# Unread products, mask steps and weight loads at the beginning of a DeltaNet and SwiGLU kernel

## Chip, core and metric

The kernel runs on one core of a Trainium2 chip. The metric is the device time of one execution in microseconds (us). The engines are named as in the profile: PE (TensorE), DVE (VectorE), ACT (ScalarE), POOL (GpSimd) and SP (SyncE, which here issues the DMAs).

## What is computed

```python
# deltanet: q, k, v of (4, 8, 768, 48), beta of (4, 8, 768)
k_n = k / (np.linalg.norm(k, axis=-1, keepdims=True) + 1e-06)
for t in range(S):
    y[:, :, t] = einsum('bhd,bhde->bhe', q[:, :, t], state)
    v_old = einsum('bhde,bhd->bhe', state, k_n[:, :, t])
    state = state + beta_t * einsum('bhd,bhe->bhde', k_n[:, :, t], v[:, :, t] - v_old)
# its output becomes x of (3072, 384); then the block with d_ff = 1536
g = x @ w_gate
out = (g / (1 + exp(-g)) * (x @ w_val)) @ w_out
```

All inputs and outputs are float32.

## The kernel before

The sequence of 768 is cut into 12 chunks of 64 positions; a chunk holds all 32 heads. For each chunk K and Q are transposed on PE (`turned`, L481), Gram products are formed (`gram_steps`, L497; `first_gram`, L638, for the first two), a small triangular matrix is inverted by substitution on DVE, and `advance` (for chunk 0 `first_advance`) applies it to V, updates the state and gives the chunk's output y. The 256 tokens of a chunk then go through the SwiGLU block: `gate_val` (products L1440, SiLU on ACT L1449, product on DVE L1451) and `output` (L1467) for the first two chunks, and forms with fewer products (L1280, L1557) for the others.

The change lies in the beginning, about the first 60 us. There chunks 0 and 1 are prepared and advanced while the weights come in. The program's order is written out by hand for all five engines, at the end of the kernel.

**Unread products.** `unread(count, p)` (L631) puts `count` products of a constant tile `half` into PSUM tile `p`, 512 columns each; nobody reads them. Before the change they stand at the very start (3) and ahead of `first_substitution` in PE's order (2). A float32 product is two weight loads and two product records in the trace.

**The first chunk.** `first_advance` has four product steps of L932, written into the banks px and py: zt with v, then n_of with v, n_of with uu, n_of with t. Between them ACT copies v and uu (L957, L967) and DVE adds into t and uu (L1510). Then come the products with `p_sb`, copies into y (L1004, L1006), transposes of y (L1018), and `of_state` (L902). `n_products` (L728) precedes them.

**Masks.** `p_sb` of chunk 0 is the Gram product of q and k (copied by ACT, L517), multiplied by a triangular mask on POOL in two halves (`under_mask`, L536). The generator `first_q[0]` yields before each half, and `next(first_q[0])` places them.

**Weight loads.** `stage(n, after)` loads piece n of the weights through SP's queue (L267). With `after` it first copies one element of piece `after` into the place of n on POOL (L266). So the load of n waits until piece `after` has landed, and POOL's queue waits with it. Pieces 0 to 23 have 256 columns of the gate and value weights, 256 KB each. `load_v` and `load_k` go through the same queue of SP.

**Conversions.** `power_step` reads a landed piece on ACT (L279, L285); `convert` finishes it on DVE with three instructions (L296, L304, L316). For the first two `gate_val` of chunk 0, `chain` stands behind each group of three products: it takes one step of `advance(1)` and converts a few pieces. `advance(1)` forms products with the state (L1054) that DVE subtracts from v (L1064), products of q (L1044), then L1073, three times L1098, `of_state` (L902) and `p_of_u` (L1127), each step between groups of L1440.

Of the kernel before, what the change touches and what calls it, by code (L numbers as in the profile page):

```python
# [13 lines left out]
C = 64  # L14
DP = 64
R = 32
# [4 lines left out]
def kernel(  # L21
# [25 lines left out]
    nc = tc.nc  # L47
# [131 lines left out]
    def load_v(c):  # L179
        vin[c] = work.tile([128, 2, NB, NJ, D], FP32, name="vin", bufs=2)  # L180
        for b in range(2):
            src = halves(v, c, b).rearrange("bp (j par) p d -> par p (bp j) d", par=2)
            for par in range(2):
                s = half_of(b ^ par if c > 1 else b).start
                nc.sync.dma_start(
                    out=vin[c][s : s + 64, par].rearrange("p bp j d -> p (bp j) d"),
                    in_=src[par],
                )
# [170 lines left out]
    def half_of(x):  # L359
        return slice(64 * x, 64 * x + 64)  # L360
# [182 lines left out]
    def gram(*args):  # L543
        for _ in gram_steps(*args):
            pass
# [82 lines left out]
    def unread(count, p):  # L628

        for _ in range(count):  # L630
            nc.tensor.matmul(p[0:R], half, half[:, 0:1].to_broadcast([128, 512]))  # L631

    def first_gram(c, tag):

        p_v = [p.rearrange("p (x h i) -> p x h i", x=2, i=R) for p in banks("p_g", tag)]
        for bp, j, par, b, _ in every():
            k_v = kt[c][half_of(par), bp, j, b].rearrange("p (x i) -> p x i", x=2)
            nc.tensor.matmul(  # L638
                p_v[par][half_of(b), :, NJ * bp + j], kt[c][half_of(par), bp, j, b], k_v
            )  # L640
        return p_v
# [66 lines left out]
    def spread_z(c, x, engine, bps=slice(0, NB)):  # L708

        def by_bp(t):  # L710
            t = t.rearrange("p (par bp j) i -> p par bp j i", par=2, bp=NB)[:, :, bps]
            return t.rearrange("p par bp j i -> p par (bp j) i")

        z_v = by_bp(first_of["z"].rearrange("p i (c h) -> p c h i", c=2)[:, c])
        out = by_bp(ztp[0][:, c, :, R * x : R * x + R])
        mask = m_rows[:, 1:2] if x else m_rows[:, 3:4]
        if engine is nc.scalar:
            nc.scalar.mul(out, z_v, mask)
        else:
            engine.tensor_scalar_mul(out, z_v, mask)  # L720
# [200 lines left out]
    def first_advance():  # L921

        zt = ztp[0][:, 0].rearrange("p (par bp j) i -> p par bp j i", par=2, bp=NB)
        r, pq = vin.pop(0), p_sb.pop(0)
        p_n = banks("p_n", 2)
        n_products(0, p_n)
        n_copies(0, p_n, (nc.scalar.copy, nc.vector.tensor_copy), nc.vector.tensor_copy)

        def product(p, at, flip, weights, moving):
            for j in range(NJ):  # L930
                for par, b in ORDER:
                    nc.tensor.matmul(  # L932
                        p[half_of(b ^ par if flip else b), at[par], j],
                        weights(par, b, j),
                        moving(par, b, j),
                    )

        def there(par, b):
            return half_of(b ^ par)

        v, uu = new_u("v0"), new_u("uu")
        t = x_flat.rearrange("p (x bp j d) -> p x bp j d", x=3, bp=NB, j=NJ)
        pairs = [
            ps_pair("p_u", tag)[:, :, 0 : NJ * D].rearrange("p x (j d) -> p x j d", j=NJ)
            for tag in ("px", "py")
        ]
        n_of = n_sb[0]
        back_of = n_back[0].rearrange("p (bp j i) -> p bp j i", bp=NB, j=NJ)
        for bp in range(NB):
            product(  # L950
                pairs[bp],
                (1, 0),
                True,
                lambda par, b, j: zt[half_of(b), par, bp, j],
                lambda par, b, j: r[half_of(b), par, bp, j],
            )
            nc.scalar.copy(v[:, :, bp], pairs[bp])  # L957
        yield MORE
        for bp in range(NB):
            product(  # L960
                pairs[bp],
                (0, 1),
                False,
                lambda par, b, j: n_of[there(par, b), par, bp, j],
                lambda par, b, j: v[there(par, b), 1 - par, bp, j],
            )
            nc.scalar.copy(uu[:, :, bp], pairs[bp])  # L967
        yield MORE
        for bp in range(NB):
            product(  # L970
                pairs[bp],
                (1, 0),
                True,
                lambda par, b, j: (
                    back_of[half_of(b), bp, j] if par else n_of[half_of(b), 0, bp, j]
                ),
                lambda par, b, j: uu[half_of(b), par, bp, j],
            )
            plus(t[:, 0:2, bp], v[:, :, bp], pairs[bp])
            for x in range(2):  # L980
                nc.scalar.copy(t[half_of(x), 2, bp], t[half_of(1 - x), 0, bp])
        yield MORE
        for bp in range(NB):
            product(
                pairs[bp],
                (0, 1),
                False,
                lambda par, b, j: n_of[there(par, b), par, bp, j],
                lambda par, b, j: t[there(par, b), 1 - par, bp, j],
            )  # L990
            plus(uu[:, :, bp], t[:, 1:3, bp], pairs[bp])
        spread_z(1, 0, nc.vector)
        load_v(2)
        yield
        y = work.tile([128, NB, NJ, 2, D], FP32, name="y", tag="r", bufs=2)
        for bp, copy in enumerate((nc.scalar.copy, nc.vector.tensor_copy)):
            product(
                pairs[bp],
                (0, 1),
                True,  # L1000
                lambda par, b, j: pq[half_of(b), par, bp, j],
                lambda par, b, j: uu[half_of(b), par, bp, j],
            )
            copy(y[:, bp, :, 0], pairs[bp][:, 0])  # L1004
            for b in range(2):
                copy(y[half_of(b), bp, :, 1], pairs[bp][half_of(1 - b), 1])  # L1006
        yield
        y_f = y.rearrange("p bp j par d -> p bp (j par d)")
        xts[0] = x_first
        p_f = [  # L1010
            p[:, 0 : KT * 128].rearrange("p (t n) -> p t n", t=KT)
            for p in banks("p_f", 2)
        ]
        x_v = x_first.rearrange("p t (bp n) -> p t bp n", bp=NB)
        for bp, copy in enumerate((nc.scalar.copy, nc.vector.tensor_copy)):
            for k in range(KT):
                at = slice(k * 128, (k + 1) * 128)
                nc.tensor.transpose(p_f[bp][:, k], y_f[:, bp, at], ident)  # L1018
            copy(x_v[:, :, bp], p_f[bp])
        p_s = of_state(0, uu)  # L1020
        spread_z(1, 1, nc.scalar)
        nc.scalar.copy(state, p_s)
        yield
# [485 lines left out]
    def plus(out, a, b):  # L1509
        nc.vector.tensor_tensor(out=out, in0=a, in1=b, op=ALU.add)  # L1510
# [296 lines left out]
    with tc.manual_schedule(  # L1807
# [28 lines left out]
        nc.vector.transpose(first_of["mb"][:, 0 : R * R], first_of["flat"])  # L1836
        r_b = first_n()
        first_scale(r_b)
        for n in range(6):
            stage(n, n - 2 if n > 1 else None)  # L1840
        load_v(1)
        turned(2, False, "py")
        first_q = [gram_steps(0, True, 0, (copy_a, copy_a))]
        next(first_q[0])
        low_copies(0, p_g[0])
        turned(3, False, "py")
        turned(1, True, "px")
        gram(2, False, "py", (copy_a, copy_a))
        low_copies(1, p_g[1])
        gram(3, False, "py", (copy_a, copy_a))  # L1850
        first_q.append(gram_steps(1, True, "px", (copy_a, copy_a)))
# [9 lines left out]
        spread_z(0, 1, nc.vector, others)  # L1861
        scale_v(0)
        next(first_q[1])
        stage(6, 4)
        next(first_q[0])
        stage(7, 5)
        next(first_q[0])
        for n in range(8, 10):
            stage(n, n - 2)
        for n in range(10, 18):  # L1870
            stage(n, n - 3)
        for n in range(18, 23):
            stage(n)
        zb_1 = work.tile([128, R, R], FP32, name="zb", bufs=1)
        new_nt(0, spare_of_q, state.rearrange("p b bp j d -> p (b bp j d)")[:, 0:512])
# [22 lines left out]
        went = []  # L1898

        def chain(_):  # L1900

            if not went:
                p_n = banks("p_n", 0)
                n_products(1, p_n)
                n_copies(1, p_n, (copy_a, copy_a), copy_a)
            step("advance", advance, 1)
            n, ahead = ((1, 7), (2, 6), (4, 4))[len(went)] if len(went) < 3 else (2, 4)
            went.append(n)
            if len(went) in (4, 5):
                next(first_q[1])  # L1910
            convert(todo[:n], ahead)
            del todo[:n]

        pairs = [(c, f) for c in range(2) for f in range(0, 8, 2)]
        pairs += [(c, f) for f in range(8, FT, 2) for c in range(2)]
# [69 lines left out]
```

## Time and profile before

| | |
|---|---|
| median of 3 runs | 687.34 us (686.76 to 689.09) |
| profiled execution, its own time | 689.76 us |
| profiled execution, span | 688.1 us |
| mean granted TensorE clock | 0.992 |
| PE busy | 653.7 us (95%) |
| DVE, ACT, POOL busy | 473.3, 256.1, 201.7 us |

The profiled execution's own time is 1.7 us longer than the span from its first to its last instruction, and 2.4 us above the median of the runs. In the profile a row gives start and duration in us, the engine, the line of the kernel, the operation with its tiles, the number of instructions merged in the row, and in brackets how long the engine had been idle and what ended that. "issue" there means that the engine waited for nothing that the profile shows.

### The profile page before, as it was taken

What the parts mean: (1) busy time and instruction counts of PE and PEld (TensorE: products, weight loads), DVE (VectorE), ACT (ScalarE), POOL (GpSimd) and SP (SyncE); (2) the same over time, 40 slices, a digit from 0 to 9 for tenths busy, and PEclk for the clock granted to TensorE, in tenths of its full rate; (3) what the DMA queues carried; (4) which work ended last, traced back from release to release, by engine and by line L of the source; (5) the groups of instructions that cost most, each with busy time, mean ns of one, the idle gap of its engine ahead of it and who ended that gap; (6) DMA issues with size and microseconds to landing.
All of it is one profiled execution on the core that took longest, in us unless ns stands there. A gap on an engine that the chain in (4) does not pass through costs nothing.

```text
span 688.1 us, 24813 instructions
## 1 busy us (share of the span) xinstructions
PE 653.7 (95%) x10850; PEld 603.7 (88%) x10850; DVE 473.3 (69%) x982; ACT 256.1 (37%) x546; POOL 201.7 (29%) x309
## 2 busy tenths in 40 slices
PE   7788999998999999999999999999999999999997
PEld 4566888756988899999999999999999999999997
DVE  7987778798569867757767747767657655645462
ACT  5785765214332332334332244332232333132130
POOL 7130031104883030881030881030882000000000
PEclk9998999999999999999999999999999999999999
DMA  9767824016226352276262176242187122132220
GB/s 135 169 176 190 243 94 137 1 35 136 45 45 164 73 136 64 49 156 143 54 134 74 45 153 138 60 110 80 26 171 152 48 88 78 40 100 71 76 71 23
DMA packets 147437, 68.55 MB, mean 100 GB/s; under 512 B 123457, under 2 KB 126561, under 8 KB 147329
## 3 DMA queue, kind: packets, MB, share of 16 engines
q1 hardware_dynamic: 144992, 66.48, 40.2%
q8 instruction: 85, 1.39, 0.8%
q10 hardware_dynamic: 2080, 0.39, 0.4%
q0 software_dynamic: 256, 0.10, 0.1%
q14 instruction: 24, 0.19, 0.1%
HBM read 59.08 MB, written 7.86 MB: 97 GB/s over the span
## 4 chain that ended last, share of the span: by engine, by line
PE 64%; DVE 3%; issue 0%; DVEq 0%
PE ffn L1280 36%; PE ffn L1557 17%; PE p_px L1073 1%; PE p_px L1054 1%; PE p_py L497 1%; PE p_py L1127 1%; PE p_py L1044 1%; DVE x_t L1510 1%; DVE ffn L1507 1%; PE p_px L902 1%; PE p_px L497 1%; PE p_py L1152 1%; PE p_py L884 1%; PE p_px L870 1%; DVE o_sb L1510 0%
## 5 line engine op out<-in xcount | busy, mean ns | idle before, releaser
L1280 PE MATMUL ffn<-x_t,w_gv 128*128 128x128 f32 x760 | 102.4, 278 | 6.6 <-DVE x_t L1507 6.6
L1280 PEld LDWEIGHTS ffn<-x_t,w_gv 128*128 128x128 f32 x760 | 93.1, 193 | 8.3 <-issue 5.8
L1557 PE MATMUL ffn<-wo_sb,h_f 128*128 128x192 f32 x480 | 84.2, 329 | 0.6 <-ACT ffn L1549 0.6
L811 POOL TENSOR_TENSOR n_b<-mb,half 128x32 f32<-128x32 f32 x5 | 27.6, 5520 | 191.3 <-DVE mb L551 191.3
L1280 PE MATMUL ffn<-x_ffn,w_gv 128*128 128x128 f32 x600 | 80.0, 277 | 0.0
L1557 PEld LDWEIGHTS ffn<-wo_sb,h_f 128*128 128x128 f32 x480 | 77.8, 190 | 1.6 <-ACT ffn L1549 0.9
L1316 ACT ACTIVATE sil<-ffn 128x256 f32<-128x256 f32 x95 | 34.5, 382 | 114.6 <-PE ffn L1280 106.6
L586 POOL TENSOR_TENSOR zb<-zb,h_f 128x31 f32<-128x31 f32 (+15 forms) x124 | 71.9, 580 | 9.7
L1280 PEld LDWEIGHTS ffn<-x_ffn,w_gv 128*128 128x128 f32 x600 | 73.8, 194 | 0.0
L580 POOL TENSOR_TENSOR h_f<-zb,mb 128x31 f32<-128x31 f32 (+15 forms) x124 | 69.4, 560 | 14.4 <-DVE mb L568 5.0
L1280 PE MATMUL ffn<-x_t,h_f 128*128 128x128 f32 x464 | 63.6, 280 | 3.9 <-DVE ffn L1507 3.9
L1317 DVE TENSOR_TENSOR h_f<-sil,ffn 128x256 f32<-128x256 f32 x95 | 37.6, 418 | 42.8 <-ACT sil L1316 42.8
L1280 PEld LDWEIGHTS ffn<-x_t,h_f 128*128 128x128 f32 x464 | 56.3, 192 | 5.9 <-DVE ffn L1507 4.9
L1440 PE MATMUL ffn<-x_ffn,w_gv 128*128 128x256 f32 x216 | 48.0, 381 | 0.0
L1440 PEld LDWEIGHTS ffn<-x_ffn,w_gv 128*128 128x128 f32 x216 | 40.7, 190 | 5.6
L1510 DVE TENSOR_TENSOR o_sb<-o_sb,ffn 128x192 f32<-128x192 f32 x49 | 17.1, 349 | 31.5 <-PE ffn L1557 31.0
L1510 DVE TENSOR_TENSOR ffn<-ffn,p_sb 128x512 f32<-128x512 f32 x36 | 24.8, 693 | 16.2 <-PE ffn L1280 15.1
L1557 PE MATMUL ffn<-last_k,h_f 128*128 128x192 f32 x200 | 35.8, 326 | 0.0
L1440 PE MATMUL ffn<-x_t,w_gv 128*128 128x256 f32 x144 | 35.7, 400 | 0.0
L1557 PEld LDWEIGHTS ffn<-last_k,h_f 128*128 128x128 f32 x200 | 32.8, 190 | 0.0
L1440 PEld LDWEIGHTS ffn<-x_t,w_gv 128*128 128x128 f32 x144 | 27.7, 199 | 4.0
L1280 PE MATMUL ffn<-x_ffn,h_f 128*128 128x128 f32 x224 | 30.0, 277 | 0.0
(343 smaller groups left out, 1165.2 us busy)
## 6 DMA issues: line engine op xcount, KB each, us to landing
h_f<-w_s SPq DMA_DIRECT2D x81, 256.0 KB, 2.7
more_w<-w_s SPq DMA_DIRECT2D x27, 256.0 KB, 2.9
vin<-in_v_dram SPq DMA_DIRECT2D x48, 96.0 KB, 3.5
out_dram<-o_sb SPq DMA_DIRECT2D x48, 96.0 KB, 2.2
kn<-in_k_dram SPq DMA_DIRECT2D x20, 192.0 KB, 4.7
w_s<-h_f SPq DMA_DIRECT2D x10, 256.0 KB, 3.2
zt<-in_moe_w_out_dram SPq DMA_DIRECT2D x6, 384.0 KB, 4.4
qpad<-in_q_dram SPq DMA_DIRECT2D x36, 64.0 KB, 3.2
```

Of the source, the lines that this page charges most:

```text
L497: nc.tensor.matmul(p_v[par][half_of(b if of_q else b ^ par), bp, j], kt[c][half_of(par), bp, j, b], xt[half_of(par), bp, j, b],)
L580: engine.tensor_tensor(out=t_v, in0=zb[:, 0 : j + 1, j : j + 1].to_broadcast([128, j + 1, m]), in1=mb[:, j : j + 1, j + 1 : R].to_broadcas ...
L586: engine.tensor_tensor(out=zb[:, 0 : j + 1, j + 1 : R], in0=zb[:, 0 : j + 1, j + 1 : R], in1=t_v, op=ALU.add,)
L811: nc.gpsimd.tensor_tensor(out=n, in0=mb.rearrange("p j i -> p (j i)")[:, 0 : R * R : R + 1], in1=half, op=ALU.pow,)
L870: nc.tensor.matmul(p_j[dst, c, m], a[lo, c, 2 * m + e, 0:R], zt[lo, c, 2 * m + e, R:C],)
L884: nc.tensor.matmul(p_j[hi, e, c, m], z1[row, c, m], t2[row, c, m])
L1280: nc.tensor.matmul(p[:, u], w(u), moving, start=start and u == 0, stop=True, skip_group_check=True,)
L1316: nc.scalar.activation(silu_of, p[:, 0:2], ACTF.Silu)
L1317: nc.vector.tensor_tensor(out=h_of(c, PAIRS[r][e % 3], e // 3), in0=silu_of, in1=p[:, 2:4], op=ALU.mult)
L1440: nc.tensor.matmul(ps[name][:, i], w_sb[:, t, (f + i) * 128 : (f + i + 1) * 128], xts[c][:, t], start=(t == 0 and i == 0), stop=(t == KT - 1),
L1510: nc.vector.tensor_tensor(out=out, in0=a, in1=b, op=ALU.add)
L1557: nc.tensor.matmul(p[x, part], a(f - f % 2)[:, f % 2], b(f), start=not begun and f == 0, stop=f == FH - 1, skip_group_check=True,)
```

## The change

Two small functions are added: `between` puts one unread product of a given number of columns into bank 0 of the FFN banks; `small_unread` puts `count` products of 64 by 64 columns of the identity. Sixteen small ones stand ahead of the transposes of K chunk 2; one long product each stands ahead of the transposes of K chunk 3, of those of Q chunk 1, and of the Gram products of chunk 3; four between the steps of chunk 0. The load of piece 5 and the loads and gates of pieces 6 to 9 are placed after both mask steps, or between them, and pieces 14 to 17 have no gate any more. In `chain`, the first call takes the step of `advance(1)` after the conversion instead of before it.

```diff
+    def between(columns):
+        p = banks("p_t", 0)[0]
+        of = half[:, 0:1].to_broadcast([128, columns])
+        nc.tensor.matmul(p[0:R, 0:columns], half, of)
+
+    def small_unread(count, p):
+        for _ in range(count):
+            nc.tensor.matmul(p[0:C, 0:C], ident[0:C, 0:C], ident[0:C, 0:C])
...
             nc.scalar.copy(uu[:, :, bp], pairs[bp])
+        between(128)
         yield MORE
...
                 nc.scalar.copy(t[half_of(x), 2, bp], t[half_of(1 - x), 0, bp])
+        between(128)
         yield MORE
...
             plus(uu[:, :, bp], t[:, 1:3, bp], pairs[bp])
+        between(256)
         spread_z(1, 0, nc.vector)
...
             copy(x_v[:, :, bp], p_f[bp])
+            if bp == 0:
+                between(256)
...
-        for n in range(6):
+        for n in range(5):
             stage(n, n - 2 if n > 1 else None)
         load_v(1)
+        small_unread(16, banks("p_t", "py")[0])
         turned(2, False, "py")
...
+        unread(1, banks("p_t", "py")[0])
         turned(3, False, "py")
+        unread(1, banks("p_t", "px")[0])
         turned(1, True, "px")
         gram(2, False, "py", (copy_a, copy_a))
+        unread(1, banks("p_t", "px")[0])
         low_copies(1, p_g[1])
...
         next(first_q[1])
-        stage(6, 4)
         next(first_q[0])
-        stage(7, 5)
+        stage(5, 3)
         next(first_q[0])
-        for n in range(8, 10):
+        for n in range(6, 10):
             stage(n, n - 2)
-        for n in range(10, 18):
+        for n in range(10, 14):
             stage(n, n - 3)
-        for n in range(18, 23):
+        for n in range(14, 23):
             stage(n)
...
-            step("advance", advance, 1)
             n, ahead = ((1, 7), (2, 6), (4, 4))[len(went)] if len(went) < 3 else (2, 4)
+            if went:
+                step("advance", advance, 1)
             went.append(n)
...
             del todo[:n]
+            if len(went) == 1:
+                step("advance", advance, 1)
```

## The prediction

> **What bounds the kernel now.** I read the page first, then PE's timeline up to 76 us, PE's waits, the windows at the points where the granted clock steps, and the DMA queues. From 64.73 us on PE hardly waits; before, it does. Whatever makes PE's first 70 us shorter is therefore carried to the end, as far as the other engines follow.
>
> ```profile
> PE   7788999998999999999999999999999999999997
> PEclk9998999999999999999999999999999999999999
> q8 instruction: 85, 1.39, 0.8%
> ```
> The fourth slice, 52 to 69 us, is the one of the first fifteen with a lower clock. Queue 8 carries PE's program: 1.39 MB in 85 packets is 16 KB each, against 21,700 PE records, so one packet holds about 256 instructions, 128 weight loads with their products.
>
> ```profile
> 31.82 0.49 PE L932 MATMUL p_px<-v,qpad 64*64 64x48 f32 x18 [1.02 <-issue]
> 35.82 0.49 PE L932 MATMUL p_px<-x_t,qpad 64*64 64x48 f32 x18 [1.02 <-issue]
> 44.34 1.15 PE L1054 MATMUL p_px<-state,kt 48*64 48x48 f32 x64 [0.51 <-issue]
> 63.70 1.10 PE L1127 MATMUL p_py<-uu,p_sb 64*64 64x48 f32 x30 [2.34 <-issue]
> ```
> These waits (and 0.58 at 48.61) have no operand behind them. Counting products from one to the next gives 128 from 31.82 to 35.82 and multiples of 128 to all the others: PE waits there for its next block of program. Blocks begin at 28.0, 31.82, 35.82, 40.2, 44.34, 48.61, 52.1, 57.5 and 63.70: where PE is dense, a block follows the one before by 4.0 to 4.3 us, and by 6.2 at the end, where loads press (the packet started 3.7 us after its block had begun, elsewhere 1.3 to 2.0).
>
> ```profile
> 15.10:18.51 3.41, 2.10 (x74) 1.00 0.94 147
> 18.51:21.93 3.42, 1.96 (x54) 1.00 0.65 119
> 59.47:62.89 3.42, 1.53 (x99) 1.00 0.89 198
> 62.89:66.30 3.41, 2.60 (x34) 0.50 0.73 151
> 66.30:69.71 3.41, 3.41 (x13) 0.50 1.07 277
> 168.70:172.11 3.41, 1.58 (x70) 1.00 0.69 233
> 172.11:175.53 3.42, 3.34 (x15) 0.50 0.01 2
> ```
> Columns: stretch, length, PE busy, granted clock, DMA share, GB/s. The clock steps on a grid of 3.41 us: after stretches 45% and 46% busy it is half, after 57% and 62% it stays full, and it returns after one 98% or 100% busy, not after 76%.
>
> **The change, part by part.** The sum is made against the profiled execution: span 688.1, own time 689.76, which is 2.42 above the median of 687.34. Two half-clock stretches lie in it; I take it that other executions catch other ones, since nothing ties the grid to the program's start.
>
> *Sixteen small products, three long ones.* L631 takes 0.45 us for a record of 512 columns, so 64 columns 0.056, and 32 records 1.8 us: from 13.43 to 15.2, over a wait of 0.87 for K. K's transposes come 0.9 late, as do the Gram products behind them. Each long one is two records, 0.9 us, in waits of 1.30, 1.46 and 1.19; the first ends at 18.2 instead of the K chunk's 17.76. The lateness is gone by 20.26, when the Q chunk lands. ACT's copy of it at 21.44 had ended its former work at 19.93, or 20.4 now; DVE's substitution, 17.04 to 25.67, needs none of it. Cost 0. Value: in this execution 0, for the clock was full here. A stretch laid at 16.5 to 19.9 holds only 1.06 us of PE work (31%), so others are halved there; this part takes that away, worth at most the 3.4 us that a stretch can lose.
>
> *Products between the steps of chunk 0.* 128 columns cost 0.22, 256 cost 0.45: 1.3 us over four places, where PE waits for ACT's copies of uu, 0.29 and 0.34 for DVE, and 0.5 for y. Over by 0.1 at the third. Cost 0.1.
>
> *Where the blocks of program fall.* The changed program has 86 more PE instructions, 74 of them ahead of the first L932, so a boundary lies 37 to 43 products earlier. I walk it with 4.0 to 4.3 per block. Blocks begin at 22.1, then 26.2 (in the Gram products of q, which had run at 25.4), so the two unread products and L728 shift from 27.78 to 28.4; 30.1 without a wait; 34.2 in the third step, 1.0 waited; 38.4 in the products with p_sb, 0.8 waited; 43.0. PE is 0.3 late at L902 (40.3 for 40.01), and gains 0.5 by L1054, where the wait at 44.34 is gone. So the two waits of 1.02 come back elsewhere and pay nothing.
>
> *Loads of weights.* Piece 5's load passes behind the four of v (2.64 us on SP's queue), 29.89 to 32.1; its first reader on ACT is at 42.65, landed by 35, cost 0. Pieces 14 to 17 lose their gate copies on POOL; the last of these stood there until 52.97 (48.97 and 4.00), with DMA at 54 GB/s from 50 to 55. Now SP issues nine loads of 256 KB in a row from 42 and v and K behind them from 46, instead of 56.9. So DMA is full from 42 to 53 and free at 57.5 to 63, the reverse of before. The block at 63.70 no longer waits: with one beginning by 57, the next is due at 61 to 62, where it is first needed. But those beginning at 43.0 and about 47.5 are fetched under load, between 4.0 and 6.2 us each. At 4.0, p_of_u (L1127) ends at 61.9; at 5.2, which I take since these loads are of long rows and only part of the time mixed with K's short ones, at 63.3; before, 64.8, or 64.25 at full clock. Of 2.34 us I keep 0.95, with bounds +2.35 and, at 6.2 each, a loss.
>
> *The clock at 62.9.* At half clock L1127's 30 records took 1.10 for some 0.55, and L1440, transposes, L1440 from 64.73 to 70.52 took 5.8 for 4.0: 2.35 us, gained if no stretch is under half busy.
>
> *Masks.* POOL's two multiplications by the mask, 1.27 each, go from 32.27 and 33.83 to about 29.1 and 30.5, behind one gate copy less each. Read at 37.18: cost 0, and DVE's L316 at 32.30, 1.52 long beside the mask and 0.42 elsewhere, shortens. PE waited for the third step, not for it: worth 0.1, which pays for the products between.
>
> *DVE's order in advance(1).* Three conversions (0.29, 0.43, 0.43) go ahead of L1064's subtraction, into the 1.82 that DVE stood idle before it. If PE's L1054 ends earlier they would delay it; it ends 0.3 earlier at most. Cost 0; DVE is 1.1 ahead behind it.
>
> *Downstream.* From 64.73 to 170.3 PE shows no wait over 0.15, so its lead counts unless DVE turns late. The nearest place is L1451 at 95.66, whose bank PE needs at 97.9: 1.5 us spare. DVE is held there by ACT, and ACT by a load landing at 78.75 after 1.99 idle; earlier loads move that. A lead of 3.3 passes.
>
> Sum: 689.76 − 0.95 − 2.35 = 686.5 with the half-clock stretch at 172.11 (3.34 us of PE work, 1.67 lost), 684.8 without. That stretch follows a wait of 1.84 and will be hit in about half of all positions of the grid. I take 684.9, near the lower one: what a median execution caught ahead of 28 us before, the long products take away, and that stands against the half of the cases in which the stretch at 172 is hit.
>
> A rule that speaks against this: the Trainium skill, TensorE: Matmul & The Clock Gate, section Why this matters for your kernels, has the clock drop only after a matmul gap of some 3 us. This trace disagrees (gap 2.34, stretch 45% busy). By that rule the fillers would buy nothing; no number above rests on it.
>
> **The rivals.**
>
> *The wait moves into the burst (slower).* The block beginning at 43.0 is followed only 6.2 later, as the one of 57.5 was: 49.2, 55.4, 61.6, needed at 46.9, 52.3 and 59.3. p_of_u ends at 67.7, 3.45 after 64.25, and these waits of 2.3 to 3.1 leave stretches under half busy, so the clock term stays. 689.76 + 3.45 − 2.42 = 690.8; I say 690.5. It decides from 5.9 per block. For it: rows near 300 GB/s go with that delay. Against: from 35 to 50 at 177 to 215 GB/s the spacing was 4.3. Chance 0.17.
>
> *An even trade (same).* One wait near 2 us at 51 takes the place of that at 61.4 and halves the clock as often: −0.95 and no 2.35, off the median: 686.4. Chance 0.23.
>
> *The wait at 63.70 is not program fetch, and stays, while the fillers act where PE has time: 687.3.* Against it: the count of 128. Chance 0.10. The Trainium skill, Runtime: NRT & Kernel Launch, section Instruction fetch mechanics, calls the cost of a 16 KB boundary mostly hidden, which this trace contradicts with 1.02, 1.02 and 2.34.
>
> *The forecast, or better.* Chance 0.50; at 4.0 per block and no stretch halved, 683.4, and if DVE's 1.1 and the earlier loads tell too, 682.
>
> **How the numbers follow.** 0.3%, about what a measurement here can tell, is 2.06 us, so faster is under 685.28 and slower over 689.40. Forecast 0.50 faster; trade and unmoved wait 0.33 same; burst 0.17 slower. The range drops the worst of the burst and less than a tenth at the lower end: 681.9 to 688.8. The forecast's own range is 682 to 685.3.
>
> **What would show it.** Right: waits of "issue" that end near 26 and 34 us instead of 31.82 and 35.82, none at 61 to 64, PEclk 1.00 from 60 to 70, DMA over 250 GB/s from 43 to 50, L481 for K at 67 to 68 instead of 70.52. Wrong: an "issue" wait over 2 us between 46 and 58, half clock from there on, PE waits on DVE L1451 near 93, or a wait for piece 5 or 7 on ACT.

## The result: 0.45% slower

The changed kernel takes 691.62 us (median of 20 runs, 687.06 to 694.70), the kernel before 688.24 (20 runs, 685.46 to 697.38). The ratio is 1.0045, with a 95% interval of 1.0023 to 1.0066. The prediction was 684.9, faster; the outcome lies above its range. Of the times on record it is nearest to that of the rival "the wait moves into the burst" (690.5), though what that rival describes happened only in part. The profiled execution of the changed kernel took 692.27 us, with a span of 690.5.

The page of the profile after, rows of the 40 slices and of the queue that carries PE's program:

```profile
PE   8888999998999999999999999999999999999997
PEclk9999999999999999999999999999999999999999
q8 instruction: 85, 1.39, 0.8%
```

PE is busier in the first two slices, which the new products fill, and the clock has no slice with an 8. Program comes in as many packets as before. By this page alone the change did what it was to do. PE's timeline shows where the waits went (start, duration, engine, line, tiles; in brackets the idle time before):

```profile
26.97 0.56 PE L497 MATMUL p_px<-qt,kt 64*64 64x64 f32 x18 [0.61 <-issue]
32.16 0.51 PE L942 MATMUL p_py<-vin,zt 64*64 64x48 f32 x21 [1.13 <-issue]
36.16 0.20 PE L942 MATMUL p_py<-uu,state 64*64 64x48 f32 x1 [1.02 <-issue]
53.63 1.07 PE L1113 MATMUL p_px<-v,zb 64*64 64x48 f32 x57 [0.73 <-issue]
59.55 1.46 PE L1455 MATMUL ffn<-x_t,w_gv 128*128 128x256 f32 x5 [1.87 <-issue]
65.67 1.11 PE L1142 MATMUL p_py<-uu,p_sb 64*64 64x48 f32 x64
70.41 1.04 PE L481 MATMUL p_px<-ident,kn 128*128 128x128 f32 x8
```

The 2.34 us ahead of `p_of_u` (now L1142) are gone, but 0.73 and 1.87 have come in ahead of 53.63 and 59.55, 5.9 us apart. K's transposes (L481) start at 70.41, where before they started at 70.52: of the 3.3 us that were to be won by then, 0.1 came. A part of that is chance: PE's very first products, which nothing changes, took 5.24 us here and 4.65 before, so the first transposes (6.20 and 5.69) were 0.51 late ahead of any change. The windows around the points where the clock steps, and two of the burst of loads (stretch, length, PE busy, the other engines, granted clock, DMA share, GB/s):

```profile
53.83:57.24 3.41, 3.41 (x128) 2.87 (x121) 1.28 (x3) 2.12 (x5) 0.00 (x0) 1.00 1.14 269
57.24:60.66 3.42, 1.55 (x10) 1.01 (x6) 3.25 (x8) 2.23 (x6) 0.00 (x0) 1.00 0.80 130
60.66:64.07 3.41, 3.41 (x69) 2.86 (x68) 1.15 (x4) 1.50 (x5) 0.00 (x0) 0.50 0.97 278
64.07:67.48 3.41, 3.41 (x136) 2.90 (x136) 3.41 (x10) 1.17 (x3) 0.00 (x0) 1.00 0.69 132
45.00:50.00 5.00, 5.00 (x236) 4.51 (x238) 4.86 (x15) 4.95 (x14) 0.18 (x1) 1.00 0.81 252
50.00:55.00 5.00, 3.77 (x112) 3.00 (x105) 3.69 (x12) 4.09 (x12) 0.00 (x0) 1.00 0.94 314
```

The wait of 1.87 leaves the stretch from 57.24 with 45% of PE work, and the next, which is full of work, runs at half clock: some 1.7 us lost, where before the two stretches from 62.89 cost 2.35. And there is something that the prediction did not look for. Behind 230 us the kernel before shows no wait of "issue" over 0.15; after, PE's timeline has two:

```profile
297.55 0.98 PE L1059 MATMUL p_py<-state,qt 48*64 48x48 f32 x51
299.50 0.44 PE L1059 MATMUL p_py<-state,qt 48*64 48x48 f32 x13 [0.98 <-issue]
558.94 1.27 PE L894 MATMUL p_py<-t,z 32*32 32x32 f32 x127
561.08 0.18 PE L894 MATMUL p_py<-t,z 32*32 32x32 f32 x1 [0.87 <-issue]
```

From the first product of chunk 3 (L1280, now L1295; 230.30 before, 230.62 after) to the end of the span it is 457.8 us before and 459.9 after. At 230 us the two executions are 0.3 us apart; 2.1 us are lost behind, 1.85 of them in these two waits.

### The profile page after: what moved, and what is told of

Read it like the earlier page. It is cut to its first block, busy times and chain, and to the rows that moved or that the text cites. A ratio compares the mean times of both kernels' runs of the same rounds, so it can differ in the third digit from the quotient of the medians.

```text
span 690.5 us, 24882 instructions
## 1 busy us (share of the span) xinstructions
PE 659.4 (95%) x10896; PEld 604.9 (88%) x10896; DVE 472.7 (68%) x982; ACT 255.7 (37%) x546; POOL 196.1 (28%) x305
## 4 chain that ended last, share of the span: by engine, by line
PE 62%; DVE 4%; issue 1%; DVEq 0%
PE ffn L1295 36%; PE ffn L1572 17%; PE p_px L1088 1%; PE p_px L1069 1%; PE p_py L1059 1%; PE p_py L1142 1%; PE p_py L497 1%; DVE x_t L1525 1%; DVE ffn L1522 1%; PE p_px L912 1%; PE p_py L1167 1%; PE p_py L894 1%; PE p_px L880 1%; PE p_px L497 1%; DVE x_t L1522 0%
## 5 line engine op out<-in xcount | busy, mean ns | idle before, releaser
L1295 PE MATMUL ffn<-x_t,w_gv 128*128 128x128 f32 x760 | 101.7, 277 | 6.3 <-DVE x_t L1522 6.3
L1295 PEld LDWEIGHTS ffn<-x_t,w_gv 128*128 128x128 f32 x760 | 92.5, 192 | 9.1 <-issue 6.7
L1295 PE MATMUL ffn<-x_ffn,w_gv 128*128 128x128 f32 x600 | 80.1, 277 | 0.0
L580 POOL TENSOR_TENSOR h_f<-zb,mb 128x31 f32<-128x31 f32 (+15 forms) x124 | 71.5, 577 | 14.4 <-DVE mb L568 5.0
L1295 PEld LDWEIGHTS ffn<-x_ffn,w_gv 128*128 128x128 f32 x600 | 73.9, 194 | 0.0
L586 POOL TENSOR_TENSOR zb<-zb,h_f 128x31 f32<-128x31 f32 (+15 forms) x124 | 69.8, 563 | 9.7
L1295 PE MATMUL ffn<-x_t,h_f 128*128 128x128 f32 x464 | 63.6, 280 | 4.2 <-DVE ffn L1522 3.9
L1295 PEld LDWEIGHTS ffn<-x_t,h_f 128*128 128x128 f32 x464 | 56.3, 192 | 6.2 <-DVE ffn L1522 4.9
L1455 PEld LDWEIGHTS ffn<-x_t,w_gv 128*128 128x128 f32 x144 | 26.9, 193 | 5.9 <-issue 2.2
L1295 PE MATMUL ffn<-x_ffn,h_f 128*128 128x128 f32 x224 | 30.6, 280 | 0.0
```

What stands on the lines that cost most here:

```text
L580: engine.tensor_tensor(out=t_v, in0=zb[:, 0 : j + 1, j : j + 1].to_broadcast([128, j + 1, m]), in1=mb[:, j : j + 1, j + 1 : R].to_broadcas ...
L586: engine.tensor_tensor(out=zb[:, 0 : j + 1, j + 1 : R], in0=zb[:, 0 : j + 1, j + 1 : R], in1=t_v, op=ALU.add,)
L1295: nc.tensor.matmul(p[:, u], w(u), moving, start=start and u == 0, stop=True, skip_group_check=True,)
L1455: nc.tensor.matmul(ps[name][:, i], w_sb[:, t, (f + i) * 128 : (f + i + 1) * 128], xts[c][:, t], start=(t == 0 and i == 0), stop=(t == KT - 1),
```

## The experiments

All theories agree that PE's waits of "issue" are waits for the next 256 instructions of its program. The packets of queue 8 bear it out: one ended at 62.25 in the kernel before, and PE went on at 63.70; one ended at 58.01 in the changed kernel, and PE went on at 59.55. At nearly all such waits in these traces 1.3 to 1.7 us lie between the two. The theories differ in which part of the change moves them to where they cost. Each ratio is against runs of the kernel before on the same chip (medians 688.46, 688.29, 688.36 and 689.21 in the four groups below). The clock is the mean over the runs; one stretch at half clock is 0.0025 of it (half of 3.41 in 688). "Behind chunk 3" is the stretch just named, from one profiled execution; the last column is the wait of "issue" between 553 and 561 us in it.

| kernel | PE instructions against before | median (runs) | ratio, 95% | clock | behind chunk 3 | wait near 558 |
|---|---|---|---|---|---|---|
| after | +86 | 691.62 (20) | 1.0045 (1.0023 to 1.0066) | 0.9943 | 459.9 | 0.87 |
| grid_before | +86 from 167 us on | 688.22 (12) | 1.0008 (0.9983 to 1.0034) | 0.9921 | 459.4 | 1.14 |
| grid_after | +256 from 169 on | 692.15 (12) | 1.0038 (1.0015 to 1.0060) | 0.9932 | 458.7 | none |
| loads_only | −4 | 688.84 (12) | 1.0008 (0.9986 to 1.0029) | 0.9922 | 457.9 | none |
| products_only | +90 | 690.37 (12) | 1.0014 (0.9992 to 1.0037) | 0.9963 | 459.9 | 1.16 |
| small_as_long | +30 | 692.43 (7) | 1.0066 (1.0037 to 1.0094) | 0.9924 | 458.3 | none |
| gates_back | +90 | 690.77 (12) | 1.0046 (1.0025 to 1.0067) | 0.9947 | 461.3 | 1.43 |
| long_only | +11 | 690.92 (12) | 1.0045 (1.0022 to 1.0068) | 0.9891 | 458.7 | none |
| gaps_filled | +55 | 690.96 (12) | 1.0033 (1.0009 to 1.0058) | 0.9920 | 458.1 | none |
| before_shifted | +84 from 285 on | 689.58 (12) | 1.0021 (0.9997 to 1.0045) | 0.9907 | 459.5 | 1.59 |
| after_shifted | +214 from 285 on | 690.25 (12) | 1.0028 (1.0000 to 1.0055) | 0.9938 | 457.5 | none |
| gates_back_shifted | +214 from 285 on | 688.17 (12) | 1.0006 (0.9981 to 1.0031) | 0.9966 | 458.9 | none |
| order_only | 0 | 687.82 (12) | 0.9997 (0.9970 to 1.0025) | 0.9912 | 457.7 | none |
| order_fill170 | +20 | 688.96 (12) | 1.0002 (0.9976 to 1.0028) | 0.9920 | 459.1 | none |
| order_long | +11 | 691.13 (12) | 1.0030 (1.0002 to 1.0058) | 0.9890 | 459.2 | none |
| gates_fill170 | +234 from 285 on | 688.41 (12) | 0.9994 (0.9964 to 1.0023) | 0.9958 | 459.0 | none |

### Which half of the change, and where the blocks lie behind 170 us

`grid_before` and `grid_after` put unread one-column products into PE's order ahead of chunk 2, so that the blocks behind lie as in the other kernel. They write into a bank in use and so spoil the output.

```diff
             if c == FAST:
+                pad(21, 1)
                 begin(c)
```

(`grid_after`: `pad(42, 1)`.) `loads_only` is the changed kernel without any of its new unread products; `products_only` is the kernel before with all of them and nothing else.

> The kernel before with 86 PE instructions added at one place, just ahead of begin(2) at 170 us, where PE waits 1.84 us anyway (21 unread products of one column and one transpose); the first 170 us are those of before. Theory of the block grid: the 256-instruction blocks of PE's program then begin 86 instructions earlier from there to the end, as in the changed kernel, and two waits of "issue" of about 1 us appear behind 175 us (at about 298 and 558 us), in all 2 to 2.5 us more than before. Rival, the later part runs slower for another reason (clock, the loads of the reloaded weights): no such waits, time as before within 0.5 us.

> The changed kernel with 170 more PE instructions at the same place (42 unread products of one column and one transpose), so that the grid from 170 us on is that of the kernel before (86 + 170 = 256). Theory of the block grid: no wait of "issue" behind 175 us, 2 to 2.5 us less than the changed kernel; what is left over before, about 1 us, is the beginning. Rival: the two waits stay near 299 and 560 us.

> The changed kernel without any of its unread products: only the masks, the order of the loads and DVE's order in advance(1) are changed, and PE's program has 4 instructions fewer than before. Theory of the burst: DMA over 250 GB/s from 43 to 55 us, a wait of "issue" of 1 us or more between 50 and 60 us in place of that of 2.34 at 61 to 64, half clock behind it in part of the executions; no waits behind 175 us. Time within 1 us of before. Rival, the unread products cause the waits at 50 to 60: none there, and 2 us or more faster than before.

> The kernel before with all of the change's unread products and nothing else of it; PE's program has 90 instructions more than before. Theory of the block grid: waits of about 1 us near 298 and 558 us, 2 to 2.5 us. Theory of the burst: no wait over 1 us between 50 and 58 us, since the loads of pieces 14 to 22 stand behind their gates as before; the wait at 61 to 64 us is gone or shorter, as its block begins 43 products earlier. In all 0 to 1 us slower than before. Rival, products in the waits of chunk 0 put off the path by themselves: L728 over 1.5 us later than in before, and over 3 us slower.

The two grid kernels were to lie 2 to 2.5 us from the kernel that each is made from; they lie 0.6 over before and 0.5 under the changed kernel, and neither difference is outside its interval. The two halves came out within their forecasts by ratio, and neither alone shows a loss outside its interval. By their traces they differ. `loads_only` has the wait in the burst, and no wait behind 230; `products_only` has none over 1 us between 45 and 170, and the one of 1.16 near 558. PE's timeline of `loads_only`:

```profile
53.62 1.02 PE L1108 MATMUL p_px<-v,zb 64*64 64x48 f32 x52
56.67 0.43 PE L1108 MATMUL p_px<-v,zb 64*64 64x48 f32 x12 [2.03 <-issue]
```

So the loads alone make the trade that the prediction had as its second rival: 2.03 at 56.67 for 2.34 at 63.70. `grid_before` got one of the changed kernel's two waits (1.14 near 556), not the one near 299. `grid_after` lost both, but its padding crossed a block boundary and waited 1.40 there itself, so that its time decides nothing.

`grid_before` also told something by accident. Its program is that of before up to 167 us, yet its timeline has no 2.34:

```profile
60.63 0.74 PE L1134 MATMUL p_py<-uu,p_sb 64*64 64x48 f32 x34
62.43 0.68 PE L1134 MATMUL p_py<-uu,p_sb 64*64 64x48 f32 x30 [1.06 <-issue]
```

In `before_shifted`, which is the kernel before up to 230 us, the same wait is 0.52. The boundary stays at the same product; how long the block is awaited changes from execution to execution, and in neither of these two is the clock halved behind it. K's transposes start at 66.72 and 67.39 in them, 3.8 and 3.1 us earlier than in the profiled execution of before, with no change ahead of them. `order_only` and `order_fill170`, alike up to 166 us, show the same spread: 0.34 and 2.37 at this boundary, the second with half clock behind it.

### Other numbers of instructions, gates back, fillers elsewhere

`small_as_long` replaces the sixteen small products with two long ones; `gates_back` gives pieces 14 to 17 their gates again; `long_only` is the kernel before with the three long products; `gaps_filled` adds to that five unread products of 128 columns among the products of `p_of_u(1)` and six ahead of chunk 2. Those in `p_of_u` share a bank with an open accumulation and spoil the output.

```diff
-        small_unread(16, banks("p_t", "py")[0])
+        unread(2, banks("p_t", "py")[0])
...
-        for n in range(10, 14):
+        for n in range(10, 18):
             stage(n, n - 3)
-        for n in range(14, 23):
+        for n in range(18, 23):
             stage(n)
```

> The changed kernel with two long unread products in place of the sixteen small ones: the same 1.8 us of PE work ahead of the K chunk, but 56 PE instructions fewer (21889 in all, 30 more than before instead of 86). Theory, the blocks of program: behind 230 us the changed kernel lost 2.4 us, in waits of 0.98 at 299.5 and 0.87 at 561, because its 86 instructions move the block boundaries so that two neighbouring blocks hold the two bursts of 128 short products near 553 and 558 and last 5.8 us together by the times of before, 1.2 less than the fetches need; with 30 more the shortest pair lasts 7.2. So no wait over 0.4 on issue behind 230, a loss of 0.4 at most there, 685.6 to 686.3 at full clock where the changed kernel's runs meet 687.6 and before's 685.0, and 689.6 to 690.4 as median, 1.0015 to 1.003. Rival, the loads: the loss is made in the burst of loads at 45 to 60 us, and the number of instructions is nothing: 691.6, 1.0045, and the loss behind 230 is an accident of that execution.

> The changed kernel with the gate copies of weight pieces 14 to 17 put back, so that these loads are not issued in one burst; all unread products stay. Theory of the blocks: the wait of 1.87 at 59.55 shrinks under 1 and the half clock at 57 to 60 becomes rarer, but the waits behind 230 (a shift of 90 instructions) remain, 1 to 2 us: 687.2 to 687.6 at full clock, median 690 to 690.8, 1.002 to 1.0035, like the products alone (690.4). Rival, the loads: the burst is the whole loss, 688.5 or under, 1.000 at most.

> The kernel before with only the three long unread products at the beginning (11 PE instructions more). Theory: the stretch at 16 to 19.9 us can no longer be halved, the mean clock rises from 0.991 to 0.993 or more, the block boundaries behind stand nearly as before (shortest pair 7.3 us), so none of the waits behind 230 comes: 685.0 to 685.4 at full clock, median 687.6 to 688.2, 0.9988 to 0.9996. Rival, the products cost path at the beginning: K and what is behind it come 0.5 to 1 later for good, 688.9 to 689.5.

> The kernel before with the three long unread products, five unread products of 128 columns (1.1 us) among the products with p_sb ahead of the block that came at 63.70, and six (1.3 us) in the wait ahead of chunk 2 at 170.4: 55 PE instructions more, each lot in a stretch where PE waits, written to columns 384 to 511 of a bank that nobody reads. Theory: no window under half busy is left between 8 us and the end, at any position of the grid, so the half clock goes, the mean clock is 0.998 or more, and the time is the full-clock time of before with at most 0.9 on it, as the shortest pair of blocks lasts 7.3: median 685.2 to 686.2, 0.9955 to 0.997. Rivals: the products in the wait delay p_of_u by their own 1.1 and chunk 2 by 0.5, 687 at a better clock, 0.998; or the clock is governed by something else and stays 0.99: 689 to 690, 1.001 to 1.002.

None of the four times came out as expected in full: the median of `gates_back` lies in its range, its ratio (1.0046 for at most 1.0035) does not; the other three are slower than forecast. Taking the burst away brought nothing against the changed kernel (1.0046 and 1.0045). The traces are clearer. With 30 instructions more (`small_as_long`) the wait near 558 is gone as the theory says, though the largest wait behind 230 is 0.49 and the loss there 0.5 (0.4 expected); but its block in the burst now ended inside L1113 and was awaited for 2.32 at 55.78, and the time is the worst of all. That it is worse than the changed kernel speaks against the theory, and I cannot explain it from one execution.

In `gates_back`, without the burst, PE's timeline has no wait between 53 and 60, where the changed kernel had 1.87, and `p_of_u` starts 4.2 us earlier than there (2.6 from the two waits, 1.6 from the clock). The loads are what moved the wait. SP's queue in the changed kernel, the last piece of the burst with the loads of v and K behind it:

```profile
50.30 0.43 SPq L267 DMA_DIRECT2D zt<-in_moe_w_gate_dram  x1
50.85 3.59 SPq L185 DMA_DIRECT2D vin<-in_v_dram  x4
54.54 2.82 SPq L139 DMA_DIRECT2D kn<-in_k_dram  x2
```

and in `gates_back`:

```profile
52.94 0.43 SPq L267 DMA_DIRECT2D zt<-in_moe_w_gate_dram  x1
53.49 3.48 SPq L185 DMA_DIRECT2D vin<-in_v_dram  x4
57.06 3.38 SPq L139 DMA_DIRECT2D kn<-in_k_dram  x2
```

Only 2.6 us lie between the two; the pieces ahead of them are spread from 43 on there, and come at 209 to 240 GB/s from 45 to 55 instead of 252 to 314.

`gates_back` keeps the wait near 558, and there it cost twice. PE's timeline, and the windows of that place:

```profile
553.54 1.25 PE L894 MATMUL p_py<-t,z 32*32 32x32 f32 x125
556.23 0.25 PE L894 MATMUL p_py<-t,z 32*32 32x32 f32 x3 [1.43 <-issue]
```

```profile
553.48:556.89 3.41, 1.98 (x134) 1.78 (x133) 0.57 (x2) 0.76 (x2) 0.00 (x0) 1.00 0.30 77
556.89:560.30 3.41, 3.41 (x19) 3.41 (x18) 1.71 (x2) 1.19 (x2) 0.00 (x0) 0.50 0.02 5
```

The 128 product records of 32 by 32, with as many weight loads, use up a block of program in 1.3 us; the next block is not there yet, and the stretch around the wait ends in half clock, which costs another 1.6.

`long_only` and `gaps_filled` refute that these fillers are free. Their clocks are no better than before's: both were at half clock from 39.0 (37.2) to 45.8 (47.5), behind a stretch in which PE waits for DVE and the program. Nor is the clock safe between 16 and 19.9 us, as was expected: in `long_only` the stretch from 15.12 to 18.53 is at half clock. Windows of `long_only`:

```profile
35.59:39.01 3.42, 1.30 (x73) 1.21 (x77) 3.35 (x8) 2.15 (x6) 1.06 (x4) 1.00 0.54 168
39.01:42.42 3.41, 3.11 (x70) 2.55 (x65) 1.81 (x5) 2.25 (x7) 0.37 (x2) 0.50 0.83 252
42.42:45.84 3.42, 3.42 (x69) 2.81 (x69) 2.87 (x7) 2.07 (x4) 1.24 (x3) 0.50 0.69 204
```

### Only the place of the blocks behind 285 us, and the rest one by one

The padding now stands in two waits for x_t, at the starts of chunks 3 and 4, in the bank that the next product clears. For `gates_back_shifted` it is `tiny(16, 0)` and `tiny(15, 1)`, for `before_shifted` `tiny(11, 0)` and `tiny(10, 1)`. `order_only` is `gates_back` without any new unread product.

```diff
+            if c == 3:
+                tiny(16, 1)
+            if c == 4:
+                tiny(16, 0)
             if c > FAST:
                 begin(c)
```

> The kernel before with 84 PE instructions more, in one-column unread products placed in PE's waits for x_t at 230 and 285 us (1.2 us each), so that from 285 on the blocks of program lie as in the changed kernel, and up to 230 as before. Theory, the blocks: a wait of 0.9 to 1.4 on issue in the burst of short products near 558 and some tenths more elsewhere, 1 to 2 us behind 285, so the mean time is 1 to 2 over before's, 0.15 to 0.3%. Rival, clock and beginning alone: the time is set by what happens ahead of 170 us, which is unchanged here: 0 to 0.1% and no wait near 558.

> The changed kernel with 128 more PE instructions in the same two waits, so that from 285 on the blocks stand 214 instructions from before's, where no two neighbouring blocks last under 7.4 us. Theory, the blocks: no wait near 558 and 0.6 at most behind 285; 1 to 2 us less than the changed kernel, 689.6 to 690.6, ratio 1.0015 to 1.003. Rival, clock and beginning alone: 691 to 692, 1.0045 as the changed kernel.

> The changed kernel with the gate copies of pieces 14 to 17 back (which ended at 690.8) and 124 more PE instructions in the two waits. Theory, the blocks: both of the change's losses are mended, the wait near 559 behind the burst of loads and the one near 558: 688.3 to 689.2, 1.000 to 1.0015, and at the clock of 0.997 and over 686 to 687.5. Rival, clock and beginning alone: 690.4 to 691.2, as without the shift.

> The changed kernel without any unread product and with the gate copies of pieces 14 to 17 back: what is left of the change is the masks ahead of the gates, piece 5 behind v, and three conversions ahead of a subtraction on DVE; the PE instructions are those of before in number. Theory: these shorten the way to 157 us by about 1 us (1.4 in the one pair of executions that shows it) and touch neither the blocks nor the clock: 687.2 to 688.2, 0.9985 to 1.000. Rival, they too shift waits into a place where the clock is halved: 689 or over, 1.001.

By their ratios all four times came out as the theory of the blocks has them (the median of `gates_back_shifted` lies 0.1 us under its range). The rows around the burst in PE's timeline of `before_shifted`:

```profile
553.95 1.29 PE L884 MATMUL p_py<-t,z 32*32 32x32 f32 x128
556.83 1.05 PE L1280 MATMUL ffn<-x_t,w_gv 128*128 128x128 f32 x8 [1.59 <-issue]
```

and of `after_shifted`:

```profile
555.80 1.29 PE L894 MATMUL p_py<-t,z 32*32 32x32 f32 x128
557.02 1.16 PE L1295 MATMUL ffn<-x_t,w_gv 128*128 128x128 f32 x8
```

The same burst, in the kernel before with 84 instructions more, is followed by a wait of 1.59; in the changed kernel with 128 more there is none. In the table the wait is there in five of five executions with a shift of 84 to 90, and in none of the twelve others (before among them). Behind chunk 3 those five take 459.4 to 461.3 us, the others 457.5 to 459.2. Other shifts have other waits, and some are as long:

```profile
509.07 0.49 PE L1290 MATMUL ffn<-x_t,h_f 128*128 128x128 f32 x3 [1.23 <-issue]
516.54 1.13 PE L1296 MATMUL ffn<-x_t,h_f 128*128 128x128 f32 x8 [1.21 <-DVE state L927]
```

The first row is of `order_long` (behind chunk 3 459.2), the second of `order_fill170` (459.1). The profile puts the second down to DVE, but a packet of program ended 1.6 us before it, and no other run has a wait over 0.3 there. `long_only`, with the shift of `order_long`, waits 0.41 at that place. So the expectation that no long wait comes where neighbouring blocks last over 7.2 us is refuted; what holds is that a shift of 84 to 90 brings the wait near 558 each time.

In time, the four pairs that differ in this alone (before and `grid_before`, before and `before_shifted`, `after_shifted` and after, `gates_back_shifted` and `gates_back`) give 0.08, 0.21, 0.17 and 0.40%, 0.22% on average or 1.5 us. The half-widths of the pairs are 0.24 to 0.35%, and only the last lies outside its own; for the average of the four I work out 0.15 from them. But `grid_after` and `small_as_long` also lack the wait near 558; the changed kernel is 0.07% slower than the first and 0.21% faster than the second. With these two the average is 0.12%, and 0 is within its interval. So the waits are shown in the traces; that they cost 1.5 us is an estimate.

The three pairs that differ in the burst (after against `gates_back`, the two shifted ones, `loads_only` against `order_only`) give −0.01, 0.22 and 0.11%. That is 0.7 us on average, no more than a hint in the times; the wait itself is shown. How far such pairs can be trusted shows in `products_only` and `gates_back`: they have the same fillers, gates and shift, and differ in the order and masks that cost nothing between before and `order_only`; yet they are 0.32% apart, and no trace says why.

### What the fillers are worth

`gates_back_shifted` has all fillers and a clock of 0.9966, `order_only` none and 0.9912, two half-clock stretches more. They take 688.17 and 687.82. In the one execution of each, `n_products` runs at 29.43 with the fillers and at 27.95 without, and K's transposes at 66.47 and 65.22: on PE's path they cost 1.25 us there. `order_only` loses 1.7 again in a half-clock stretch from 168.74, which the fillers do not reach, and at chunk 3 the two are level (225.73 and 225.79). Three more kernels ask why. `order_fill170` puts five products of 128 columns ahead of chunk 2 into `order_only`, `gates_fill170` into `gates_back_shifted`; `order_long` is `order_only` with the three long products.

```diff
             if c == FAST:
+                beside(5, "py")
                 begin(c)
```

> The kernel called order_only with five unread products of 128 columns (1.1 us, 20 PE instructions) in PE's wait for x_t ahead of chunk 2, at 166 to 168 us. Theory: the window ahead of 168.7 is then 80% busy, so the half-clock stretch behind it (dense work, 1.7 us lost, in over half of all positions of the grid) never comes: the mean clock goes from 0.991 to 0.993, the median from 687.8 to 686.8 to 687.3, ratio 0.998 to 0.9995. Rival: the products wait for ACT's copy of x and end after x_t is there, so chunk 2 starts some tenths late and eats the gain: 687.8 to 688.3, 1.000.

> order_only with the three long unread products at the beginning (12 PE instructions). Theory: alone on the kernel before they lost 0.45% because the blocks then fell so that one was awaited for 2.3 us at 57.5 and the clock was halved at 39, not by their own work: here 687.5 to 688.6, 0.999 to 1.001, with no wait on issue over 1.3. Rival: the three products themselves cost it, by delaying K and all behind it by 1 to 1.5 us: 689.7 to 691, 1.003 to 1.0045, whatever the waits are.

> The kernel called gates_back_shifted with the five products of 128 columns in the wait ahead of chunk 2. Theory: mean clock 0.998 instead of 0.9966, and as a stretch there costs 1.7 us where it comes, 687.2 to 687.8 as median, 0.9985 to 1.000. Rival as above, the products themselves delay chunk 2: 688.2 to 688.8.

The three long products lose again, 0.30% here and 0.45% in `long_only`, both outside the interval and against the theory. The ratio of `order_long` is that of its rival, the products' own delay (1.003 to 1.0045). In all three profiled executions that have them without the products between the steps of chunk 0 (`long_only`, `gaps_filled`, `order_long`) PE is at half clock for two to four stretches between 33 and 47 us; in the others this comes in two of fourteen. Windows of `order_long`:

```profile
29.98:33.39 3.41, 1.84 (x111) 1.59 (x107) 3.10 (x5) 1.93 (x6) 3.08 (x5) 1.00 0.53 143
33.39:36.80 3.41, 2.82 (x99) 2.53 (x90) 1.79 (x6) 2.51 (x7) 0.08 (x1) 0.50 0.79 174
36.80:40.21 3.41, 3.21 (x112) 3.10 (x116) 2.52 (x5) 1.55 (x5) 0.37 (x2) 0.50 0.50 147
40.21:43.63 3.42, 3.11 (x59) 2.22 (x54) 1.82 (x5) 2.96 (x7) 0.48 (x3) 0.50 0.68 195
43.63:47.04 3.41, 3.41 (x46) 2.75 (x42) 3.27 (x8) 2.28 (x6) 1.28 (x3) 0.50 0.54 142
```

A stretch 54% busy is followed by half clock, and stretches 83, 94 and 91% busy do not end it; the full one does. So the place where the clock falls decides what it costs. Behind the K wait of the beginning one such stretch costs next to nothing: with it (15.14 to 18.56) `n_products` runs at 27.95 in `order_only`, without it at 27.90 in `loads_only`. Between 33 and 47 us half clock lasts for up to 13.7 us. Why it comes there with the long products is open: `n_products` is later (28.45 in `order_long`, 27.95 in `order_only`), but 0.37 of these 0.50 stand at the first transposes already (6.21 and 5.84), ahead of the long products, so the delay of 1 to 1.5 that the rival asked for is not in the trace; the boundaries move by 11 instructions; and no run tells the two apart.

`order_fill170` and `gates_fill170` have no half clock at 166 to 177, as expected, and no gain that their intervals could show. The first (1.0002) came out as its rival says; of the second the ratio (0.9994) is in the range of the theory, the median (688.41) in that of the rival. No version here beats the kernel before by more than a measurement can tell; `order_only`, `gates_back_shifted` and `gates_fill170` equal it and, by their ratios, lie 0.39 to 0.51% (2.7 to 3.5 us) under the changed kernel.

## Why the prediction was wrong, step by step

- **The walk of the blocks.** It expected boundaries near 26.2, 30.1 (no wait), 34.2 and 38.4; waits came at 26.97, 32.16 and 36.16 (0.61, 1.13, 1.02). That the two waits of 1.02 only change place was right. The failing step stands under Downstream: "From 64.73 to 170.3 PE shows no wait over 0.15, so its lead counts unless DVE turns late." The prediction looks no further than that. The 86 instructions move the boundaries through the remaining 500 us too, and the kernel before lies where no burst of short products falls into a block of its own. This term, left out of the sum, is 2.1 us in the profiled execution and 1.5 on average over four pairs (0.8 over the six).
- **The burst of loads.** Taken: 5.2 us from block to block under load, keeping 0.95 of 2.34. Measured: 4.9 and then 5.9 from 48.7 to 53.63 to 59.55, and 2.60 of waits in place of 2.34. The rival had set its turning point at 5.9. The rate was as forecast (252 and 314 GB/s); the price of it was mis-sized. That the time came near the rival's 690.5 is luck: it had 6.2 from block to block and three waits of 2.3 to 3.1.
- **The gain of 0.95 itself.** It was taken against the 2.34 of one execution. The same program waited 1.06 and 0.52 there in two others. The base of this term was a draw, not a property of the kernel. The whole sum starts from that execution, 2.42 over the median; the 3.3 us that the change was to win by K's transposes are what two other executions of the unchanged beginning have by themselves (3.1 and 3.8).
- **The clock at 62.9.** The 2.35 us were counted as won; the wait in the burst brought the half clock back at 60.66, for some 1.7 us. The trade, of which the second rival spoke, is what `loads_only` does.
- **Sixteen small and three long products at cost 0.** `n_products` runs at 29.30 instead of 27.78 (28.4 forecast). Of these 1.5 us, 0.51 stand at the first transposes and 0.61 are the wait at 26.97. The lateness that was to be gone by 20.26 is not: Q's transposes run at 21.12 instead of 20.29, for the small products took 2.08 us, not 1.8, and each long one 1.05, not 0.9. In the times, the price of all fillers is met by the gain: `gates_back_shifted` and `order_only` differ by 0.35 us. But the gain was not 0 by clock (two stretches fewer), so the cost was not 0 either; and long products alone lose 0.30 to 0.45%.
- **Masks, DVE's order, piece 5.** Cost 0 holds within what the times can tell: `order_only` is at 0.9997 (0.9970 to 1.0025).
- **The stretch at 172.** Half clock there (173.30 to 176.71) came as the prediction allowed. Filling it brought nothing measurable. The last 1.6 us of the forecast (686.5 to 684.9) stood on this stretch staying at full clock, and no part of the change acts on it.

Why the gain of 3.3 did not come is shown: the wait and its half clock moved. Why the kernel is slower by 3.1 us (0.45%) is shown in part. By the pairs about 1.5 go to the shifted blocks and 0.7 to the burst, both estimates; the rest is within what these pairs leave uncertain, and is not assigned.

The Trainium skill (Runtime: NRT & Kernel Launch, section Instruction fetch mechanics) calls the cost of crossing a 16 KB boundary mostly hidden. In the changed kernel's trace that is so for all of some 85 boundaries but eight; one costs 0.26, the others 0.6 to 1.9 us each, 7.2 together. So the prediction's word that its trace contradicts the page goes too far: five boundaries showed a wait there. But where the few fall is what separates the two executions behind 230 us.

## What to carry to other kernels

Where a tuned kernel streams its program in blocks, instructions added at its beginning move every boundary behind them: walk the blocks to the end of the program, and look for bursts of short instructions that fill a block by themselves. A wait of one execution is not yet a term of a sum; where another execution of the same program is to be had, compare it first: here the same unchanged beginning took 66.7 to 70.5 us up to K's transposes. Ask of a filler not only whether it hides in a wait but what it shifts: its count of instructions can cost more than its time.

## What was not expected of the hardware

- A block whose 256 instructions are 128 products of 32 by 32 lasts 1.3 us; in five executions the next came 2.3 to 3.1 us after such a block had begun, though DMA was little loaded (77 GB/s in the window of `gates_back`). There the packet started at 553.33 and took 1.45 us, and PE went on 1.45 behind its end.
- Half clock outlasts its cause: behind 54% it stayed for four stretches, and ended only after one that was 100% busy.
- The edge is not a plain share of busy time: 57% in the kernel before (18.51 to 21.93) kept the clock, 58% in `gates_back` (553.48 to 556.89), most of it products of 32 by 32, lost it. The Trainium skill (TensorE: Matmul & The Clock Gate, section Why this matters for your kernels) has the drop follow a gap of about 3 us; the longest gap there was 1.43.
